# Loading the second batch's rows before the second weights of expert 3, with a margin for the sums of weights

## The chip, the cores and the metric

The kernel runs on one core of one Trainium2 chip. The metric is the device time of one execution in microseconds (us). The profile of each kernel is of one execution. The kernel before took 372.05 us in the median of the first three runs.

## The reference

The reference does two things one after the other: attention with a sliding window of 128 and four sink positions, and a mixture of four experts over all tokens, whose weights depend on the domain and not on the token's content.

```python
def _attn_ref(q, k, v, n_sink, window):          # B, H, S, D = 4, 8, 768, 64
    scores = scale * np.matmul(q, k.transpose(0, 1, 3, 2))
    keep = is_sink | in_window                   # 4 sinks, or 0 <= row - column < 128
    a = softmax of the kept scores               # written out in the original
    return np.matmul(a, v)

def _moe_ref(x, domain_probs, w1, w2):           # 3072 tokens, 512 wide, E = 4, F = 1024
    p = domain_probs / (domain_probs.sum(-1, keepdims=True) + 1e-09)
    for e in range(E):
        h = np.maximum(x @ w1[e], 0.0)
        out += p[:, e:e + 1] * (h @ w2[e])
```

The output of the attention, with heads side by side, is the input x of the mixture.

## The kernel before

The program is written by a scheduler in Python that is run once, when the kernel is built. It keeps a clock of its own (`t`, in ns) for each engine, estimates with it when data will have landed, and chooses by these estimates what TensorE does next. So there are two orders to watch. One is the order of the loads. The other is the order of the instructions on TensorE and VectorE, which follows from the estimates. A change in the first changes the estimates and so the second, although nothing is said about it in the code.

At the start of the main part, TensorE does the mixture of batch 0 while the inputs of batch 1 come in: rows of q and k (`load_nat`), a transposition of them by DMA (`turn_nat`), v (`load_v`). A batch has 768 rows, six blocks of 128; the kernel works in groups of two blocks, so I speak of the first, second and third pair. For some products the kernel also needs sums and differences of weights (`weight_form`, L294 to L300) and of tokens (L1052), which VectorE makes, and which are queued when the clock says that their inputs have landed.

```python
# --- the scheduler's own clock and its estimates, in ns ---
    t = {"pe": 1200.0, "act": 0.0, "dve": 0.0, "pool": 1280.0, "sp": 800.0, "sw": 6500.0, "hw": 0.0}
    ring, whole = [0.0] * 6, [False] * 6
    WARM = 6600.0
    FLIP, LATE = 300, 2500
    # ... cut ...
    def lands(key, rows, cols, *deps):
        issued = pool(0, *deps, fixed=880)
        t["sw"] = max(t["sw"], issued + 1500) + rows * ROW[cols] / 16
        landed[key] = t["sw"] + 900

    def sp(*deps, issue=530, takes=600):
        t["sp"] = max([t["sp"], *deps]) + issue
        at = max(t["hw"], t["sp"] + 800)
        t["hw"] = at + takes + max(0.0, min(takes, t["sw"] - at))
        return t["hw"] + 900
    # ... cut ...
# --- loads (gpsimd queue) and transpositions (sync queue) ---
    def load_nat(b, tb):
        both = sb.tile([P, 2, H, D], BF16, name="qkn", tag="qkn", bufs=NQB)
        for i, src in enumerate((q, k)):
            nc.gpsimd.dma_start(
                out=both[:, i], in_=src[b, :, tb * P:(tb + 1) * P, :].rearrange("h p d -> p h d"),
            )
            lands(("qk", b, tb), H * P, D, qkn_free[0])
        qkn_free.pop(0)
        qkn_free.append(1e12)
        nat[b, tb] = both

    def turn_nat(b, tb):

        if b not in qkT:
            qkT[b] = sb.tile([P, 2, NHP, S], BF16, name="qkT", tag="qkT", bufs=1)
        nc.sync.dma_start(
            out=qkT[b][:, :, :, tb * P:(tb + 1) * P].rearrange("c i h p -> c (i h) p"),
            in_=nat[b, tb].rearrange("p i h d -> p (i h d)"), transpose=True,
        )
        turned_at[b, tb] = sp(landed["qk", b, tb], scored_at.get(b - 1, 0.0), issue=1330, takes=1400) + LATE
        qkn_free.remove(1e12)
        qkn_free.append(turned_at[b, tb])
        qkn_free.sort()
    # ... cut: load_first, casts ...
    def load_v(b, ts):
        for tb in ts:
            nc.gpsimd.dma_start(
                out=vx[tb][:, :, 0:D],
                in_=v[b, :, tb * P:(tb + 1) * P, :].rearrange("h p d -> p h d"),
            )
            lands(("v", b, tb), H * P, D, values_at[b - 1, min(NG - 1, (tb + 1) // 2)] if b else 0.0)

    w1_sb, w2_sb = {}, {}
    # ... cut: load_w1, of the same kind ...
    def load_w2(e):
        w2_sb[e] = wpool.tile([P, NFB, Dout], BF16, name=f"w2_{e}", tag=f"w2_{e}")
        nc.gpsimd.dma_start(out=w2_sb[e], in_=moe_w2[e].rearrange("(fb p) d -> p fb d", p=P))
        lands(("w2", e), F, Dout)
    # ... cut ...
# --- sums of weights on VectorE: when may one be queued ---
    def form1_due(e):
        n = formed1.get(e, 0)
        if e >= OWN and turned_at.get((B - 1, NQB - 1), 1e12) > t["pe"]:
            return False
        return landed.get(("w1", e), 1e12) < t["pe"] and (n < 3 or n == 3 and not left1[e])

    def form_due(e):
        n = formed.get(e, 0)
        return landed.get(("w2", e), 1e12) < t["pe"] and (n < 3 or n == 3 and e in used)
    # ... cut ...
    def next_form():

        if forming:
            return False
        x = next(((weight_form1, e) for e in FAST if form1_due(e)), None) or next(
            ((weight_form, e) for e in range(E) if form_due(e)), None)
        if x is None:
            return False

        def run(engine):
            forming.clear()
            x[0](x[1])
        forming.append(x)
        later("dve", t["pe"], 9000, run)
        return True

    forms_at = {}
    # ... cut ...
# --- differences of tokens (only the test that the argument touches) ---
            at = max(xT_at.get((b, hp, g), 1e12) for hp in range(NHP))
            if at > t["pe"]:
                return
    # ... cut ...
# --- main loop: what is loaded, and when ---
        if not att.more() and not loaded:
            loaded = 1
            gates_by_row()
            loads += [(load_w1, 3), (load_w2, 3)]
            turns += [(1, tb) for tb in range(NQB)]
            for tb in range(NQB):
                loads.append((load_nat, 1, tb))
                if tb % 2:
                    loads += [(load_v, 1, (tb - 1,)), (load_v, 1, (tb,))]
        if loads and t["pool"] < now + 1500 and load_ready(loads[0]) < now + 1500 and free_ring(loads[0]):
            x = loads.pop(0)
            x[0](*x[1:])
        if turns and (ahead < 2 or not mix.second) and landed.get(("qk", *turns[0]), 1e12) < now and (turns[0][0] <= ahead or turns[0][0] == ahead + 1 and not att.todo):
            x = turns.pop(0)
            turn_nat(*x)
            # ... cut: queueing of the next batch ...
        flush(now)
        mix.tokens()
        mix.chore()
        if ahead:
            next_form()
        # ... cut: choice of the next step for TensorE ...
```

The softmax here doesn't subtract the row's maximum and nothing guards it: scores larger than these inputs give would overflow.

## Time and profile before

| kernel before | value |
|---|---|
| first three runs | 370.67 to 372.08 us, median 372.05 |
| profiled run | 369.88 us (span 368.1 us) |
| TensorE (PE) busy in the span | 357.2 us, 97% |
| w2 of expert 3 (w2[3]) landed | 61.38 us |
| last rows of batch 1 landed, transposed | 82.80, 87.49 us |

The page, the chain, TensorE's timeline and the stages are shown in the prediction below, and are not shown again. What they leave out is the short list of what TensorE waited for between 60 and 120 us, in the waits view of the kernel before. The columns are the engine, what waited, what ended the wait, and then the total in us, the number of waits, and the longest.

```profile
PE sinks L581 <- DMA qkT<-qkn: 0.7, 1, 0.7
PE acc L1303 <- DVE H L1015: 0.3, 1, 0.3
PE hps L1000 <- ACT aT L645: 0.2, 1, 0.2
PE acc L1303 <- issue: 0.2, 1, 0.2
```

(One more line, 0.2 us before the score products L620, on ScalarE, is cut.) The longest is the sinks' wait on the transposed rows. The last line has no releaser, only "issue"; its run of 512-column products at 83.92 us is x7, so one record is missing from it, and it is no wait. This view counts the time in which TensorE was idle; the 1.09 us of the prediction counts from the end of streaming of the product before, which is a little earlier than the modelled end of that product (by about 0.3 us at the last sinks). Below, "wait" means the second of these unless I say idle.

### The profile page before, as it was taken

The numbers are of one execution on the slowest core, as the hardware profiler recorded it, in microseconds if no ns is written. First come the engines' busy times: TensorE is split into PE (matmuls) and PEld (weight loads), VectorE is DVE, ScalarE is ACT, GpSimd is POOL, SyncE is SP. The second block draws the span as 40 slices with busy tenths as digits, with TensorE's granted clock in tenths as the row PEclk, the third lists the DMA queues.
The fourth block names the chain that finished last, engine by engine and source line by source line (L and its number), as shares of the span: only waits on it lengthen the run. The fifth ranks groups of instructions, "written<-read, shape, count | busy, mean of one in ns | idle before, by whom it ended". The sixth has DMA issues, their size and how long they took to land.

```text
span 368.1 us, 9866 instructions
## 1 busy us (share of the span) xinstructions
PE 357.2 (97%) x4107; PEld 297.1 (81%) x4119; DVE 283.3 (77%) x629; ACT 154.3 (42%) x397; POOL 71.2 (19%) x92
## 2 busy tenths in 40 slices
PE   6899999998999999999999999999999999999996
PEld 2575766765776788898888898899999999999995
DVE  5674997566543899789879979869898988898860
ACT  4764723369547155456444545452103213223110
POOL 8945113604901920010020000000000000000000
PEclk9999999999999999999999999999999999999999
DMA  9999999998999991518792131213002111020011
GB/s 164 173 189 199 210 212 179 144 147 143 167 159 231 176 150 31 86 46 86 142 147 73 16 102 30 45 45 86 16 19 85 30 45 60 16 74 2 2 59 57
DMA packets 117288, 37.20 MB, mean 101 GB/s; under 512 B 100612, under 2 KB 112740, under 8 KB 117244
## 3 DMA queue, kind: packets, MB, share of 16 engines
q0 software_dynamic: 77520, 17.31, 53.9%
q1 hardware_dynamic: 38668, 18.75, 23.6%
q8 instruction: 32, 0.52, 0.6%
q10 hardware_dynamic: 1056, 0.52, 0.5%
q14 instruction: 12, 0.10, 0.1%
HBM read 40.45 MB, written 6.34 MB: 127 GB/s over the span
## 4 chain that ended last, share of the span: by engine, by line
PE 69%; DMA 19%; POOL 5%; DVE 4%; issue 2%; ACT 1%; POOLq 0%; SPq 0%; DVEq 0%
PE acc L1232 29%; PE cps L1078 20%; PE hps L1000 13%; DMA w<-in_moe_w_dram 12%; DMA qkn<-in_k_dram 4%; PE acc L1303 3%; POOL qkn L191 2%; DMA xT<-onat 2%; PE od L686 2%; PE sps L620 2%; DMA qkT<-qkn 1%; POOL vx L256 1%; POOL w L269 1%; DVE H L1024 1%; PE od L679 1%
## 5 line engine op out<-in xcount | busy, mean ns | idle before, releaser
L1000 PE MATMUL hps<-xT,w 128*128 128x256 bf16 x768 | 95.0, 273 | 0.4 <-ACT aT L645 0.2
L1000 PEld LDWEIGHTS <-w 128*128 128x128 bf16 x768 | 73.0, 98 | 13.4 <-issue 2.2
L1232 PEld LDWEIGHTS <-H 128*128 128x128 bf16 x600 | 56.0, 98 | 6.5 <-issue 0.8
L645 ACT ACTIVATE aT<-sps 128x512 bf16<-128x512 f32 (+1 forms) x96 | 47.0, 579 | 26.7 <-PE sps L620 26.7
L1078 PEld LDWEIGHTS <-w 128*128 128x128 bf16 x768 | 48.3, 98 | 2.0 <-issue 0.5
L1232 PE MATMUL acc<-w,H 128*128 128x256 bf16 x360 | 48.0, 273 | 0.0
L725 ACT ACTIVATE onat<-od,R 128x64 bf16<-128x64 f32 x144 | 33.8, 327 | 32.6 <-DVE R L713 30.6
L1303 PE MATMUL acc<-w,H 128*128 128x512 bf16 x180 | 44.2, 379 | 1.1 <-issue 0.3
L1097 DVE SCALAR_TENSOR_TENSOR H<-cps,gates 128x512 bf16<-128x512 f32 x57 | 38.6, 683 | 2.2 <-PE cps L1078 1.2
L1275 ACT COPY osb<-acc 128x256 f32<-128x256 f32 x36 | 13.5, 375 | 58.2 <-PE acc L1232 56.0
L1013 ACT ACTIVATE H<-hps 128x512 bf16<-128x512 f32 x39 | 23.2, 599 | 34.5 <-PE hps L1000 34.3
L1024 DVE SCALAR_TENSOR_TENSOR H<-hps,gates 128x512 bf16<-128x512 f32 x44 | 30.0, 686 | 9.3 <-PE hps L1000 9.1
L256 POOL DMA_DIRECT2D vx<-in_v_dram x24 | 21.4, 909 | 60.4 <-PE od L686 49.2
L1303 PEld LDWEIGHTS <-H 128*128 128x128 bf16 x192 | 17.9, 98 | 18.6 <-DVE H L1015 0.8
L1232 PE MATMUL acc<-wf,H 128*128 128x256 bf16 x240 | 31.9, 273 | 0.0
L1232 PEld LDWEIGHTS <-S 128*128 128x128 bf16 x288 | 27.0, 98 | 3.1 <-issue 0.3
L1078 PE MATMUL cps<-T,w 128*128 128x128 bf16 x384 | 29.3, 219 | 0.0
L1078 PE MATMUL cps<-xT,w 128*128 128x128 bf16 x384 | 29.1, 219 | 0.0
L1106 ACT COPY cps<-cps 128x512 f32<-128x512 f32 x24 | 13.8, 576 | 33.1 <-PE cps L1078 31.0
L1078 PEld LDWEIGHTS <-vf 128*128 128x128 bf16 x432 | 26.9, 98 | 1.0 <-issue 0.3
L639 DVE TENSOR_TENSOR aT<-aT,mask 128x1024 bf16<-128x1024 bf16 (+1 forms) x36 | 22.7, 638 | 5.3 <-ACT aT L645 5.3
L1315 DVE SCALAR_TENSOR_TENSOR osb<-acc,scale_t,osb 128x512 f32<-128x512 f32 x18 | 13.5, 749 | 15.2 <-PE acc L1303 14.3
(116 smaller groups left out, 514.2 us busy)
## 6 DMA issues: line engine op xcount, KB each, us to landing
w<-in_moe_w_dram POOLq DMA_DIRECT2D x7, 1024.0 KB, 18.9
out_dram<-osb SPq DMA_DIRECT2D x23, 256.0 KB
gates<-gate_rows SPq DMA_DIRECT2D x36, 128.0 KB
vx<-in_v_dram POOLq DMA_DIRECT2D x24, 128.0 KB, 8.2
qkn<-in_q_dram POOLq DMA_DIRECT2D x22, 128.0 KB, 7.3
qkn<-in_k_dram POOLq DMA_DIRECT2D x22, 128.0 KB, 7.6
w<-in_moe_w_dram POOLq DMA_DIRECT2D x2, 512.0 KB, 8.3
kraw<-in_k_dram ACTq DMA_DIRECT2D x2, 256.0 KB
```

The source lines that it names most:

```text
L256: nc.gpsimd.dma_start(out=vx[tb][:, :, 0:D], in_=v[b, :, tb * P:(tb + 1) * P, :].rearrange("h p d -> p h d"),)
L639: nc.vector.tensor_mul(a, a, m[:, None, :].to_broadcast([P, 2, w]))
L645: nc.scalar.activation(out=a[:, ph], in_=sps[ph][:, 0:w], func=AF.Exp, scale=scale)
L725: nc.scalar.mul(o[:, qi, hp, ph * D:(ph + 1) * D], od[:, qi, ph, 0:D], R[:, qi, ph])
L1000: nc.tensor.matmul(h[:, i].rearrange("p (q n) -> p q n", q=2), lhsT=w1_sb[e][:, db, fb * P:(fb + 1) * P], rhs=xT[b, g][:, :, db], start=(i ...
L1013: nc.scalar.activation(out=dst, in_=h, func=AF.Relu)
L1024: nc.vector.scalar_tensor_tensor(out=dst, in0=h, scalar=0.0, in1=gate, op0=ALU.max, op1=ALU.mult,)
L1078: nc.tensor.matmul(y[:, f], lhsT=A[:, d, f * P:(f + 1) * P], rhs=T[:, d], start=(m in ("P1", "P5") and f == 0 and d == 0), stop=(d == 1), ...
L1097: nc.vector.scalar_tensor_tensor(out=dst, in0=src, scalar=0.0, in1=gate, op0=ALU.max, op1=ALU.mult)
L1106: nc.scalar.copy(out=tiles["Y"], in_=y)
L1232: nc.tensor.matmul(x, lhsT=self.operand(b, g, e, m)[:, f], rhs=forms[e][m][:, f], start=(k == 0 and f == 0 and m in (("P1", "P5", "P2") if ...
L1303: nc.tensor.matmul(op, lhsT=H[:, fb // QF, fb % QF, s], rhs=w2_sb[e][:, fb, :], start=(fb == 0), stop=(fb == NFB - 1),)
```

## The change

The intent: the rows and v of batch 1 are what the attention of batch 1 waits for, while w2[3] is needed only late, so the rows go first. Since w2[3] then lands later, the sums of its parts must not be queued before it is there: VectorE works in order, and a sum that stands on its weights holds all that is behind it. Therefore the diff also asks that a landing lies 4 us back on the scheduler's clock before a sum is queued.

```diff
--- before.py
+++ after.py
@@ -335,11 +335,11 @@
         n = formed1.get(e, 0)
         if e >= OWN and turned_at.get((B - 1, NQB - 1), 1e12) > t["pe"]:
             return False
-        return landed.get(("w1", e), 1e12) < t["pe"] and (n < 3 or n == 3 and not left1[e])
+        return landed.get(("w1", e), 1e12) + 4000 < t["pe"] and (n < 3 or n == 3 and not left1[e])
 
     def form_due(e):
         n = formed.get(e, 0)
-        return landed.get(("w2", e), 1e12) < t["pe"] and (n < 3 or n == 3 and e in used)
+        return landed.get(("w2", e), 1e12) + 4000 < t["pe"] and (n < 3 or n == 3 and e in used)
 
     forming = []
 
@@ -1367,12 +1367,13 @@
         if not att.more() and not loaded:
             loaded = 1
             gates_by_row()
-            loads += [(load_w1, 3), (load_w2, 3)]
             turns += [(1, tb) for tb in range(NQB)]
+            loads.append((load_w1, 3))
             for tb in range(NQB):
                 loads.append((load_nat, 1, tb))
                 if tb % 2:
                     loads += [(load_v, 1, (tb - 1,)), (load_v, 1, (tb,))]
+            loads.append((load_w2, 3))
         if loads and t["pool"] < now + 1500 and load_ready(loads[0]) < now + 1500 and free_ring(loads[0]):
             x = loads.pop(0)
             x[0](*x[1:])
```

## The prediction

> **What bounds the kernel now.** I read the page first (busy shares and the chain that ended last), then the chain in order of time between 27 and 92 us, then TensorE's and ScalarE's timelines there, and last the instruction order of the changed program against that of the kernel before. The page:
>
> ```profile
> PE 357.2 (97%) x4107; PEld 297.1 (81%) x4119; DVE 283.3 (77%) x629; ACT 154.3 (42%) x397; POOL 71.2 (19%) x92
> ...
> PE 69%; DMA 19%; POOL 5%; DVE 4%; issue 2%; ACT 1%; POOLq 0%; SPq 0%; DVEq 0%
> ```
>
> TensorE is busy in 97% of the span and holds 69% of the chain, but DMA holds 19%, so it looks as if earlier loads could pay. The chain in order of time shows where that DMA share lies:
>
> ```profile
> 29.98 31.40 DMA w<-in_moe_w_dram
> 61.38 0.28 issue
> 61.66 0.88 POOL qkn L191
> ...
> 69.08 13.72 DMA qkn<-in_k_dram
> 82.80 0.02 SPq L203
> 82.82 0.03 issue
> 82.85 4.64 DMA qkT<-qkn
> 87.49 0.14 issue
> 87.63 0.29 PE sinks L581 x4
> ```
>
> The second weights of expert 3 (I call them w2[3]) land at 61.38 us; behind them come the rows of batch 1, the last at 82.80; their transposition lands at 87.49; then TensorE may do the sink scores of batch 1. This is the load whose place the change alters. But a chain names one path, not how long TensorE waited on it. That is in TensorE's timeline (start, length, work, and in brackets the idle time before):
>
> ```profile
> 78.62 1.03 PE L1000 MATMUL hps<-xT,w 128*128 128x256 bf16 x8 [0.24 <-ACT aT L645]
> ...
> 83.09 0.67 PE L620 MATMUL sps<-qkT 64*128 64x128 bf16 x12 [0.15 <-ACT onat L725]
> 83.92 1.67 PE L1303 MATMUL acc<-w,H 128*128 128x512 bf16 x7 [0.16 <-issue]
> ...
> 86.33 0.55 PE L620 MATMUL sps<-qkT 64*128 64x128 bf16 x6
> 87.63 0.29 PE L581 MATMUL sinks<-qkT,ksd 128*32 128x256 bf16 x4 [0.75 <-DMA qkT<-qkn]
> ```
>
> The longest gap is the one on the transposed rows, and the others are on ScalarE. Between 61 and 75 us TensorE never waits: while w2[3] loads it does mixture work of batch 0. Stages of 5 us (busy time of PE, PEld, DVE, ACT, POOL) say why it waits on ScalarE:
>
> ```profile
> 80.00:85.00 5.00, 4.69 (x62) 3.49 (x61) 3.28 (x10) 4.95 (x20) 0.00 (x0) 1.00 1.82 182
> 85.00:90.00 5.00, 4.25 (x48) 2.27 (x47) 3.73 (x7) 4.99 (x16) 2.15 (x4) 1.00 0.64 113
> ```
>
> ScalarE is full (4.95 and 4.99 of 5.00) because attention of batch 1, late by then, is emitted almost without mixture work in between.
>
> **What can be won at all.** The program order of the changed kernel has exactly the same number of products of each shape, so the streaming time does not change. Start to start, a 256-column product takes 109 ns, a 128-column one 56, a 512-column one 216: 768 + 1008 of the first, 1344 of the second and 192 of the third are 193.6 + 75.3 + 41.5 = 310 us, and the attention products come on top. I took every gap from one start to the next less these times. From 40 to 366 us about 11 us are left. Gaps of 216 ns inside a run of 512-column products are records missing from the trace (the run is x7 instead of x8), and each visit to the half-height score products costs about 0.10 us going in and 0.11 coming out. What is left as true waiting after 75 us and up to 120 is: 1.09 us before the sinks at 87.63 (the six score products before it end streaming at about 86.5); on ScalarE 0.32 + 0.22 + 0.29 + 0.19 = 1.0 us, from the gaps before 78.62, 83.09, 83.92 and 91.65; and 0.48 us near 111 us, on VectorE. Together 2.6 us, 0.7% of the time. After 120 us nearly all of the remaining gaps are the visits to the score products.
>
> **What the Trainium skill says.** TensorE: Matmul & The Clock Gate, "Wait — 56ns, not 53.3ns?": a warm matmul starts N / 2.4 GHz + about 2.5 ns after the one before. The trace agrees (56, 109, 216 ns), so a group at this spacing has nothing to win. PSUM — Partial Sum Buffer, "Engine vs sequencer instructions": VectorE's queue is strict FIFO, so a sum whose weights have not landed holds up all evictions behind it. In the trace before this cannot be seen for w2[3], whose first sum starts at 64.59, 3.2 us after the landing. DMA: Bandwidth & Descriptors, "Issuing engines are not separate DMA queues": all loads run on the same 16 engines. The trace agrees: rows that land about 0.9 us apart while the queue is alone take 1.6 us and more apart when the transpositions run beside them. TensorEngine Tiling (Array Packing), "Key Properties": a change of tiling mode drains TensorE, which fits the 0.2 us per visit.
>
> **The change part by part.** (1) Rows and v of batch 1 go ahead of w2[3]. GpSimd's timeline has issues at 36.75, 41.97, 46.82, 51.83, 56.54 and 61.66 us, each let go by the landing of one weight transfer: a weight of 1 MB takes 4.7 to 5.2 us of the queue. So all 18 transfers of batch 1 move ahead by about 5.1 us: the last row from 82.80 to 77.7, its transposition from 87.49 to 82.4, and that of the second row block from 75.8 to 70.7. The changed order has the first scores 6.07 us of streaming time earlier in TensorE's program (24 products of 256 columns, 2.61 us, and 16 of 512, 3.46 us, now stand behind them), so at about 77.71 - 6.1 = 71.6 us: 0.9 us after their rows. The last sink scores stand 6.25 us of streaming later, near 92 us, ten us after their rows. So the 1.09 us wait goes entirely. The sinks and scores of the second group come at about 77.3 us against a landing at about 77.1: that can turn into a new wait of up to 1 us.
>
> (2) Attention is moved, hardly thinned. From the first scores to the last of the second group the changed order has 9.6 us of streaming, before 10.5; the mixture work in between is the same, four groups of eight 256-column products and two of eight 512-column ones, 6.9 us. ScalarE's program in that part is 8 exponentials at 0.40, 8 at 0.53, 20 small scalings at 0.235, a sink row 0.4 and one eviction 0.6: 3.2 + 4.2 + 4.7 + 0.4 + 0.6 = 13.1 us. TensorE, with about eight visits of 0.2 us, needs 9.6 + 1.6 = 11.2 us. So ScalarE stays full there and the fourth score pair, which needs its banks, waits near 83 us for about as long as before: of the 1.0 us I leave 1.0 us standing. Only after it, where the last two sinks used to follow, is there now mixture work.
>
> (3) w2[3] lands later. It starts when v is through, at 84.07 - 5.1 = 79.0, takes 5 us, and shares the engines with the last row transposition and that of the first attention output, about 2 us: 86 us. TensorE's first use of it (second products of expert 3) stands at the same place as before, about 101 us, so it has 15 us to spare. VectorE's first sum of it stands behind the fourth mask of the second group and is reached, with ScalarE as the pace (71.6 + 0.4 + 13.1, and a mask), near 85 us. The margin of 4 us in the queueing rule is counted on the program's own clock; by my estimate it falls short by about 1 us. VectorE then stands for that time, and TensorE, which still has free banks, loses perhaps 0.3 us of it.
>
> (4) The rest of the margin only delays sums of expert 0 to 2 by a step or two; nothing moves in TensorE's order for it. From the second products of expert 3 on, TensorE's order of the two programs is the same apart from one pair of scores, so what is won by 100 us is kept to the end.
>
> Sum: waits of 2.6 us become 0.48 (near 111 us, same order) + 1.0 (ScalarE) + 0.3 (second group of rows, an even chance of some 0.5) + 0.3 (VectorE behind w2[3]), near 2.0. The gain is 0.6 us; the three runs before have a median of 372.05 and a mean of 371.60, and from the middle of the two, 371.8, I come to 371.2 us.
>
> **The rivals.** First: the whole shift counts. The chain runs through the rows, they land 5.1 us sooner, so the kernel ends 5 us sooner, at 367. For it speaks the chain; against it that TensorE waited only 1.09 us for them, and that its streaming is fixed. The most it could gain, with every wait after 75 us gone, is 2.6 us: 369.4. Second: w2[3] lands much later than estimated, at 90 us or after, because of the transpositions beside it. VectorE then stands 5 us in its strict order with all reciprocals and evictions behind it, both accumulators fill, and TensorE loses 3 to 4 us: net 2 us slower, 374. For it speaks how the rows slowed (16 us for the last ten rows and v, where 9 would do); against it that most of the transpositions are over by 82 us. Third: nothing, because the new waits eat the old: 372.
>
> **Range and chances.** Central 371.2. Three runs of the kernel before spread over 1.4 us, and the rivals reach from 369.4 to 374, with the second less likely; 8 in 10 between 369.2 and 372.9. Faster by 2% needs 7.4 us where only 2.6 us of waits exist: 0.02. Slower by 2% needs VectorE held for over 8 us: 0.02. Within 2%: 0.96.
>
> **What would show it.** In the changed profile: first scores of batch 1 near 71.6 us; rows all landed near 78 us and w2[3] near 86; no wait of the sinks on transposed rows at the end of the burst; ScalarE still full (over 4.8 of 5 us) between 74 and 85, and some 2 us of TensorE waits there in place of 2.6; TensorE's second products of expert 3 starting 0.3 to 1.5 us sooner than 102.57. Step (3) is right if VectorE shows an idle stretch of 1 to 3 us before a sum of w2[3] (line 294), released by the weight transfer; wrong if there is none or if it exceeds 4 us. I am wrong as a whole if waits appear after 105 us that were not there, where both programs have the same order.

## The result, and the profile after

| | this (us) | range | before in the same rounds (us) | ratio |
|---|---|---|---|---|
| changed kernel | 369.66 | 369.15 to 370.00 | 371.83 | 0.9947 [0.9921, 0.9972] |

Ratios in this document are computed as the mean time of one kernel's runs over that of the other's of the same rounds, so they are not quite the ratio of the medians that stand beside them. By the ratio the changed kernel is half a per cent faster, about 2.0 us. The result was correct.

The profiled run of the changed kernel took 370.0 us, at the slow end of its runs, and that of the kernel before 369.88, at the fast end of its own. The two traces therefore do not show the gain as a difference of spans (368.3 and 368.1 us). They show the mechanism. First the page of the changed kernel, busy time and chain by engine:

```profile
PE 358.1 (97%) x4119; PEld 296.8 (81%) x4119; DVE 283.0 (77%) x629; ACT 154.4 (42%) x397; POOL 71.3 (19%) x92
...
PE 74%; DMA 17%; POOL 4%; DVE 3%; issue 1%; ACT 1%; POOLq 0%; DVEq 0%; SPq 0%; ACTq 0%
```

TensorE is as full as before. The chain goes from 69% on TensorE to 74%, and from 19% on DMA to 17%: a shift of several per cent in the chain, for half a per cent of time. The chain in order of time (start, length, what) shows where it leaves the transfers:

```profile
29.97 27.39 DMA w<-in_moe_w_dram
57.36 0.28 issue
...
59.52 9.84 DMA qkn<-in_k_dram
...
69.41 9.28 DMA qkT<-qkn
78.69 0.14 issue
78.82 0.32 PE sinks L581 x4
```

Before, the chain waited on weights until 61.38 us, and on rows until 87.49. Now the weights let go at 57.36 and the rows at 78.69, and it is the second pair of row blocks that the chain waits for, at the first sinks, not the last pair at the last sinks. TensorE's timeline shows both sinks (in brackets the idle time before):

```profile
71.66 0.51 PE L620 MATMUL sps<-qkT 64*128 64x256 bf16 x8
...
78.82 0.29 PE L581 MATMUL sinks<-qkT,ksd 128*32 128x256 bf16 x4 [1.59 <-DMA qkT<-qkn]
...
82.27 1.03 PE L1000 MATMUL hps<-xT,w 128*128 128x256 bf16 x8 [0.44 <-ACT onat L725]
...
94.82 0.29 PE L581 MATMUL sinks<-qkT,ksd 128*32 128x256 bf16 x4
```

The wait at the last sinks is gone: they come at 94.82, and their rows were there at 88.15. In exchange the first sinks wait 1.66 us (1.59 of it idle), where in the profiled run of the kernel before they did not wait. (They only just did not: their rows landed at 82.19 and they started at 82.35.) The stages in the same columns as in the prediction:

```profile
75.00:80.00 5.00, 3.41 (x39) 1.88 (x38) 1.90 (x7) 2.49 (x11) 0.00 (x0) 1.00 1.82 149
80.00:85.00 5.00, 4.56 (x52) 3.04 (x51) 3.01 (x6) 5.00 (x19) 0.00 (x0) 1.00 1.22 197
85.00:90.00 5.00, 5.00 (x53) 3.79 (x52) 3.02 (x6) 3.31 (x11) 1.50 (x3) 1.00 0.92 143
```

ScalarE is full from 80 to 85 us, but not from 74 on, as was predicted: from 75 to 80 it is busy for 2.49 us, since it idles 2.51 us until the first sinks give it their scores at 79.22. After 85 it is full no more (3.31 of 5.00, before 4.99), and TensorE is busy in all of 85 to 90. Last, VectorE's timeline around the landing of w2[3] at 87.00 us:

```profile
86.82 0.69 DVE L639 TENSOR_TENSOR aT<-aT,mask 128x1024 bf16<-128x1024 bf16 x1 [0.17 <-ACT aT L645]
87.43 0.68 DVE L294 TENSOR_TENSOR wf<-w 128x1024 bf16<-128x1024 bf16 x1
88.03 0.18 DVE L713 RECIPROCAL R<-od 128x4 f32<-128x4 f32 x1
90.57 0.29 DVE L1052 TENSOR_TENSOR T<-xT 128x256 bf16<-128x256 bf16 x1 [2.37 <-DMA xT<-onat]
```

The first sum of w2[3] (L294) started 0.43 us after the landing, with no idle time before it. The margin sufficed, barely: in the two copies the sum starts 0.45 and 0.03 us after the landing. VectorE does stand for 2.37 us, but before a difference of tokens, on the transposed output of the attention; TensorE's timeline has no wait that follows from it.

### The profile page after: what moved, and what is told of

Same layout as the page of the kernel before. It is cut to its first block, busy times and chain, and to the rows that moved or that the text cites. A ratio compares the mean times of both kernels' runs of the same rounds, so it can differ in the third digit from the quotient of the medians.

```text
span 368.3 us, 9878 instructions
## 1 busy us (share of the span) xinstructions
PE 358.1 (97%) x4119; PEld 296.8 (81%) x4119; DVE 283.0 (77%) x629; ACT 154.4 (42%) x397; POOL 71.3 (19%) x92
## 4 chain that ended last, share of the span: by engine, by line
PE 74%; DMA 17%; POOL 4%; DVE 3%; issue 1%; ACT 1%; POOLq 0%; DVEq 0%; SPq 0%; ACTq 0%
PE acc L1232 29%; PE cps L1078 20%; PE hps L1000 15%; DMA w<-in_moe_w_dram 11%; PE acc L1303 5%; DMA qkn<-in_k_dram 3%; DMA qkT<-qkn 3%; PE od L686 2%; PE sps L620 2%; POOL qkn L191 1%; POOL vx L256 1%; PE od L679 1%; ACT onat L725 1%; DVE H L1024 1%; POOL w L279 0%
## 5 line engine op out<-in xcount | busy, mean ns | idle before, releaser
L1000 PE MATMUL hps<-xT,w 128*128 128x256 bf16 x768 | 95.3, 273 | 0.4 <-ACT onat L725 0.4
L1000 PEld LDWEIGHTS <-w 128*128 128x128 bf16 x768 | 72.8, 98 | 13.8 <-issue 2.7
L1303 PE MATMUL acc<-w,H 128*128 128x512 bf16 x192 | 45.4, 379 | 0.0
L639 DVE TENSOR_TENSOR aT<-aT,mask 128x1024 bf16<-128x1024 bf16 (+1 forms) x36 | 22.7, 641 | 7.3 <-ACT aT L645 7.3
```

Source lines behind the costliest of these rows:

```text
L639: nc.vector.tensor_mul(a, a, m[:, None, :].to_broadcast([P, 2, w]))
L1000: nc.tensor.matmul(h[:, i].rearrange("p (q n) -> p q n", q=2), lhsT=w1_sb[e][:, db, fb * P:(fb + 1) * P], rhs=xT[b, g][:, :, db], start=(i ...
L1303: nc.tensor.matmul(op, lhsT=H[:, fb // QF, fb % QF, s], rhs=w2_sb[e][:, fb, :], start=(fb == 0), stop=(fb == NFB - 1),)
```

## The experiments

Twelve kernels ran, in three calls of four, each call on one chip with runs of the kernel before among them. All results were correct. To compare what the traces lose and gain I also use the time from TensorE's 193rd to its 385th 256-column product of L1000, which start at 64.1 to 66.4 us and at 122.5 to 131.1. The work between these is the same in all the kernels, and it holds everything that the change moves.

| label | what it is | this (us) | before (us) | ratio [95%] | stretch (us) |
|---|---|---|---|---|---|
| (first profile) | before | | | | 58.23 |
| (first profile) | changed | 369.66 | 371.83 | 0.9947 [0.9921, 0.9972] | 58.40 |
| c_before | copy of before | 371.12 | 370.54 | 1.0004 [0.9978, 1.0031] | 58.86 |
| c_after | copy of changed | 369.81 | 370.54 | 0.9971 [0.9954, 0.9989] | 58.08 |
| e_order | loads moved, no margin | 377.18 | 370.54 | 1.0170 [1.0146, 1.0194] | 67.02 |
| e_margin | margin, loads not moved | 370.83 | 370.54 | 0.9996 [0.9975, 1.0016] | 59.95 |
| e_blate | before, rows estimated 2 us later | 368.92 | 370.64 | 0.9949 [0.9926, 0.9973] | 57.16 |
| e_m2 | changed, margin of 2 us | 375.12 | 370.64 | 1.0133 [1.0102, 1.0164] | 62.09 |
| e_mid | changed, w2[3] after row block 4 | 376.55 | 370.64 | 1.0143 [1.0114, 1.0173] | 64.81 |
| e_late3 | changed, later rows estimated 2 us later | 371.05 | 370.64 | 1.0009 [0.9982, 1.0037] | 61.13 |
| e_late3t | e_late3, token differences queued later | 368.03 | 370.88 | 0.9922 [0.9897, 0.9946] | 56.23 |
| c_after2 | copy of changed | 370.27 | 370.88 | 0.9986 [0.9961, 1.0010] | 58.69 |
| e_blate2 | e_blate again | 368.96 | 370.88 | 0.9950 [0.9926, 0.9973] | 57.14 |
| e_bl4 | before, rows estimated 4 us later | 368.84 | 370.88 | 0.9938 [0.9912, 0.9964] | 57.13 |

My theory was that the gain is the wait on the rows, less a new and smaller one. The rivals were that the gain comes from the sums' new places on VectorE and not from the loads; that it is only a matter of runs; and, later, that it comes from the place of the attention in TensorE's program and not from the rows landing sooner.

### c_before: the kernel before once more

No edit. It was to show how much the waits of one program vary from run to run.

> The kernel before, unchanged, against itself, for a second trace and the noise of a ratio. Theory A (the gain is the wait of the last sink scores of batch 1 on their transposed rows, and its size varies from run to run with the landing of the rows): ratio 1.000 within 0.003; in the trace the last transposed rows land later than the 87.49 us of the first trace, by some 1 to 2 us, and the wait before the sinks is longer by the same amount than the 1.09 us there; the span is longer than 368.1 us by about as much. Theory B (the runs differ by their first 40 us, and the measured gain of 2.2 us is partly luck): the sinks are reached with a wait near 1.1 us as before, and a longer span comes from the stretch up to 40 us.

The time is that of the kernel before, as it should be: 1.0004. The trace is not. Its timeline of TensorE has both sinks waiting:

```profile
83.84 0.29 PE L581 MATMUL sinks<-qkT,ksd 128*32 128x256 bf16 x4 [0.64 <-ACT onat L725]
...
89.57 0.29 PE L581 MATMUL sinks<-qkT,ksd 128*32 128x256 bf16 x4 [1.43 <-DMA qkT<-qkn]
```

The last sinks wait 1.43 us idle (1.75 from the end of streaming) where the first profile had 0.75 (1.09), and the first sinks 0.71 where it had none. The rows landed later: w2[3], ahead of them in the queue, at 63.13 us here and at 61.38 in the first profile. (The view puts the first of these waits on ScalarE. The transposition of the fourth block landed at 83.70, and the sinks started 0.14 us after it, as in the other traces; ScalarE's scalings ended just then, at 83.81, but in the first profile the same sinks started at 82.35 with these scalings running until 83.04, so they do not need the last of them. It is the rows.) So the prediction, which took its removable wait from a single trace, took it from a lucky one. The difference between the two runs is there early: the first landing of weights is at 16.30 us in the first profile and at 17.57 here, and lies between 16.22 and 17.77 in all traces. What makes it so stays open. Of the 1.4 us by which this span is longer, 0.8 us are there before the stretch begins (at 66.24, not 65.46) and 0.6 are in it, so both theories of the expectation have a part.

### c_after and c_after2: the changed kernel twice more

No edit. One copy ran in the first call and one in the third, beside the experiments that they are compared with.

> The changed kernel, unchanged, timed in more rounds, with a second trace. Theory A: 0.993 to 0.997 of the kernel before; a wait of 0.5 to 2 us before the first sinks of batch 1 (on the second pair of row blocks) and none before the last. Theory B: 0.997 to 1.001, and the wait of the first sinks is about as large as the one removed.

> The changed kernel again, on the same chip as the two beside it: 0.994 to 0.998 of the kernel before, a wait of 1.3 to 1.8 us before the first sinks, runs within 1 us.

Three calls give the ratios 0.9947, 0.9971 and 0.9986; the first two exclude 1, the third does not. Their mean is 0.9968, about 1.2 us. The traces agree with the first one: the last sinks do not wait in any of the three, the first sinks wait 1.66, 1.28 and 1.46 us. The runs of the changed kernel also agree better with one another (369.71 to 370.10 us) than those of the kernel before (369.62 to 372.87 for its copy). In the third call they do not agree within 1 us as expected (369.81 to 371.38), and the ratio 0.9986 is outside the expected 0.994 to 0.998.

### e_margin: the margin alone

The kernel before with the two `+ 4000` and with its own order of loads.

```diff
-        return landed.get(("w2", e), 1e12) < t["pe"] and (...)
+        return landed.get(("w2", e), 1e12) + 4000 < t["pe"] and (...)    # and the same for w1
```

> Only the margin, loads in their old order. TensorE's order is that of the kernel before instruction for instruction; five sums on VectorE move by a few places near 65 us, where VectorE is idle for a third of the time. Theory A: ratio 1.000 within 0.003. Theory D (the margin by itself gives the gain): 0.993 to 0.997.

The ratio is 0.9996: the margin by itself gives nothing. TensorE's order is exactly that of the kernel before, and five sums moved on VectorE. Its trace is also a third look at the waits of that order: 1.21 us at the first sinks, 1.58 at the last. The theory that the sums' new places make the gain falls.

### e_order: the moved loads alone

The changed kernel without the two `+ 4000`.

```diff
-        return landed.get(("w2", e), 1e12) + 4000 < t["pe"] and (...)
+        return landed.get(("w2", e), 1e12) < t["pe"] and (...)           # and the same for w1
```

> Only the loads moved, without the margin. VectorE's first sum of the second weights of expert 3 now stands nine instructions earlier, ahead of an eviction of an accumulator and of the last three masks of the second group. Theory A (the margin is what keeps VectorE from standing in front of a load that has not landed): VectorE idles 4 to 8 us before that sum until the landing near 87 us, TensorE loses 3 to 6 us of it, and the kernel is slower than the changed one by that and slower than before by 1 to 4 us: 1.003 to 1.010. Theory C (the margin does nothing, VectorE has slack): equal to the changed kernel within 0.002, 0.993 to 0.997.

It is 1.7% slower than the kernel before, more than the 0.3 to 1.0% that was expected, and 7.4 us slower than the copy of the changed kernel (377.18 less 369.81). VectorE's timeline says why:

```profile
86.49 0.69 DVE L294 TENSOR_TENSOR wf<-w 128x1024 bf16<-128x1024 bf16 x1 [9.62 <-DMA w<-in_moe_w_dram]
```

The first sum of w2[3] was queued too early, and VectorE stood 9.62 us on it. A mask of the attention (L639) stood behind it, and TensorE needed that mask, as its timeline shows:

```profile
88.50 0.40 PE L686 MATMUL od<-vx,aT 128*128 128x65 bf16 x4 [4.96 <-DVE aT L639]
89.04 5.02 PE L1000 MATMUL hps<-xT,w 128*128 128x256 bf16 x24
```

TensorE waited 4.96 us and then did 24 products in 5.02 us, for which it takes 2.78 at its usual pace: another 2.2 us. (The mean granted clock of this run was 0.991: it was 0.50 from 86.81 to 93.63 us.) The Trainium skill, TensorE: Matmul & The Clock Gate, "What's actually happening", says that the clock of TensorE falls back to 1.2 GHz, half of its full rate, after an idle window of about 3.4 us; this trace agrees, with a gap of 4.96 us: 5.02 us for 24 products is 209 ns each, where 2.78 us is 116. 4.96 and 2.2 are nearly the whole loss. The margin alone is worth nothing, but with the moved load it is what keeps the change from being a loss of 6.6 us.

### e_m2: half the margin

```diff
-        ... + 4000 < t["pe"] ...
+        ... + 2000 < t["pe"] ...
```

> The changed kernel with a margin of 2 us in place of 4. The first sum of the second weights of expert 3 stands behind the first mask and the eviction that ended at 82.8 us in the changed kernel, ahead of two evictions and three masks. Theory A: VectorE idles 3.5 to 5 us before it, until about 87 us; TensorE loses 1 to 3.5 us and some more where its granted clock falls: 1.000 to 1.008 of the kernel before, between the changed kernel and the one without margin. Theory C (a threshold lies below 2 us): as the changed kernel, 0.994 to 0.998.

A margin of 2 us is not enough: 1.0133, above the expected 1.000 to 1.008. VectorE stands 4.3 us before L294 (a line of its waits view), and TensorE waits for an eviction that stands behind it (its timeline):

```profile
DVE wf L294 <- DMA w<-in_moe_w_dram: 4.3, 1, 4.3
```

```profile
88.18 1.91 PE L1000 MATMUL hps<-xT,w 128*128 128x256 bf16 x16 [3.52 <-DVE H L1015]
```

Here 16 products after 3.52 us of idleness took 1.91 us, the usual pace, so this run did not pay with its clock (its mean granted clock was 1.0). It was the fastest of its runs (373.33 us, where the others go up to 377.43). The others have no trace, but the record gives their mean granted clock: 0.990 to 0.995 in all five. So most runs of this kernel did pay with the clock as well. Between a margin of 4 us and one of 2 us lies a loss of 1.6% (from 0.9971 in the first call to 1.0133 here); where in between it begins was not tried, and the two ratios are of different calls.

### e_mid: w2[3] in the middle of the rows

If w2[3] were loaded after four of the six row blocks, VectorE would have it sooner and the first two pairs would still be early. The experiment also asks what a transfer of 1 MB beside the transpositions does to them.

```diff
         for tb in range(NQB):
             ...
                 if tb % 2:
                     loads += [(load_v, 1, (tb - 1,)), (load_v, 1, (tb,))]
+                if tb == 3:
+                    loads.append((load_w2, 3))
-            loads.append((load_w2, 3))
```

> The changed kernel with the second weights of expert 3 loaded between the fourth and the fifth row block of batch 1, not behind the sixth. They should land 8 to 10 us sooner, near 77 to 79 us; the last rows land 5 us later but their sinks have 6.7 us of slack in the changed kernel's trace. Theory A: the first sinks wait as in the changed kernel (1.2 to 1.9 us), the last do not, VectorE stands at most 1.5 us for the weights: 0.994 to 0.999. If all rows must be ahead for the gain, a wait of over 1 us before the last sinks and 0.999 to 1.004.

It is 1.4% slower, which neither of the two expectations foresaw: w2[3] landed at 81.87 us instead of 77 to 79, VectorE stood 4.09 us for it, and the long wait came before the first sinks, not the last. The chain in order of time, and TensorE's timeline where it ends:

```profile
68.71 14.79 DMA qkT<-qkn
83.50 0.14 issue
```

```profile
83.64 0.41 PE L581 MATMUL sinks<-qkT,ksd 128*32 128x256 bf16 x4 [6.30 <-DMA qkT<-qkn]
...
84.52 3.60 PE L1303 MATMUL acc<-w,H 128*128 128x512 bf16 x8
```

The transposition of the fourth row block took 14.79 us, and landed only after w2[3]. The same block took 9.3 us in the changed kernel, beside loads of rows and v alone; the shortest transpositions in the traces take 3.1 us (one in the kernel before runs from 108.92 to 112.02). The sinks waited 6.30 us for it, and again the products after that ran at half the pace (3.60 us for eight of 512 columns, usually 1.89). In the changed kernel the same is seen in the fifth block: issued at 76.18, when its rows had landed, and itself landed at 87.29, 11.1 us later and after w2[3] at 87.00; in the kernel before the same block took 5.8 us. So of the two later places that were tried, the last one, which the change chose, is where w2[3] does the rows less harm.

### e_blate, e_blate2 and e_bl4: only the scheduler's estimate

The loads and the rule for sums stay those of the kernel before; what is changed is that the scheduler believes that the transposed rows of batch 1 land 2 us later (4 us in e_bl4). No transfer moves earlier. The attention of batch 1 only comes later in TensorE's program, behind mixture work.

```diff
-        turned_at[b, tb] = sp(landed["qk", b, tb], scored_at.get(b - 1, 0.0), issue=1330, takes=1400) + LATE
+        turned_at[b, tb] = sp(landed["qk", b, tb], scored_at.get(b - 1, 0.0), issue=1330, takes=1400) + LATE + (2000 if b == 1 else 0)
```

> The kernel before with its loads and sums as they were; only the program's own estimate of when a transposition of batch 1's rows lands is set 2 us later, so the scheduler puts the first sink scores 1.9 us and the last 3.8 us of streaming later in TensorE's order. Theory A (the kernel before loses time because TensorE's order reaches the sinks before the rows, by 1.1 to 2.9 us in its traces): no wait of the sinks on transposed rows over 0.3 us, 0.993 to 0.998 of the kernel before, and runs that agree within 1 us. Theory E (the earlier loads give something else, which a later place in the order can't): 0.998 to 1.003, with new waits, or the same on ScalarE.

> The kernel before with the estimate for batch 1 set 2 us later, again, beside the changed kernel on one chip. Theory A (both take away the same waits): both ratios between 0.993 and 0.998 and within 0.002 of each other. If moving the loads gives something more: the changed kernel ahead by over 0.002.

> The kernel before with the estimate for batch 1 set 4 us later. Theory A: no wait of TensorE on transposed rows in any case, even where the rows land 2 us later than in the first trace, and attention of batch 1 still early enough for what follows: 0.993 to 0.998. If attention is then too late for the first units of batch 1: a wait of TensorE after 105 us and 0.998 to 1.003.

The ratios are 0.9949, 0.9950 and 0.9938. TensorE's timeline of e_blate has the sinks without a wait:

```profile
85.03 0.29 PE L581 MATMUL sinks<-qkT,ksd 128*32 128x256 bf16 x4
...
91.64 0.29 PE L581 MATMUL sinks<-qkT,ksd 128*32 128x256 bf16 x4
```

What the waits view still lists from 60 to 120 us is 0.4 us on ScalarE (in e_bl4, 0.5 on VectorE at 110.48). The runs of e_blate agree less well than expected: within 1.7 us, not 1. So no load has to move to get the gain. These two kernels are ahead of the copy of the changed one (0.9950 and 0.9938 against 0.9986). The 95% intervals just overlap, so the times alone do not settle that they are faster. The stretch gives 57.14 and 57.13 us against 58.69; the 1.5 us between are about what the first sinks wait in the changed kernel (1.46 in that trace). I had expected the estimate alone to come within 0.002 of the change, and it came out 0.0036 ahead, most likely for that reason. I read the change in the same way, which is an inference: it too puts the attention further behind the rows that it needs, by moving the rows instead. It does not get all of the gain: its first sinks come too soon. That is tested next.

### e_late3: the first sinks of the changed kernel, later

If that is so, the changed kernel should gain by an estimate that is 2 us later for the blocks from the third on, so that the sinks wait no more.

```diff
-        turned_at[b, tb] = sp(landed["qk", b, tb], scored_at.get(b - 1, 0.0), issue=1330, takes=1400) + LATE
+        turned_at[b, tb] = sp(landed["qk", b, tb], scored_at.get(b - 1, 0.0), issue=1330, takes=1400) + LATE + (2000 if b == 1 and tb > 1 else 0)
```

> The changed kernel, with the estimate of when the transpositions of the third to sixth row block of batch 1 land set 2 us later; the first sinks move 2.6 us of streaming later. Theory A: their wait of 1.3 to 1.7 us goes, 0.990 to 0.996 of the kernel before and 1 to 1.7 us faster than the changed kernel. Rival F: VectorE's order now has the token differences of the first attention output, which landed at 90.6 us in the changed kernel, ahead of the fourth mask; it stands for it 2 to 4 us and TensorE gives the gain back: 0.996 to 1.001.

It did not gain: 1.0009. The wait of the first sinks is gone, but TensorE has new ones, 1.8 us on a mask and 1.2 us on an eviction, both of VectorE. VectorE's timeline shows what both stood behind:

```profile
90.76 0.29 DVE L1052 TENSOR_TENSOR T<-xT 128x256 bf16<-128x256 bf16 x1 [5.08 <-DMA xT<-onat]
90.97 0.68 DVE L639 TENSOR_TENSOR aT<-aT,mask 128x1024 bf16<-128x1024 bf16 x1
```

The first difference of tokens (L1052) was now queued ahead of the mask, and stood 5.08 us on the transposed output of the attention, which was issued at 84.00, while w2[3] was still loading (it landed at 87.22), and landed at 90.74. In the changed kernel the same difference stood 2.37 us, but with nothing urgent behind it. The two new waits are not all: from 94.31 to 97.72 us the granted clock of this trace is 0.50, and 16 products from 94.25 take 3.55 us instead of 1.91. No single gap before it was longer than 1.75 us; from 90.90 to 94.31 TensorE was idle for 2.00 us in all. The trace is of the slowest run of this kernel (373.03 us, median 371.05), so its stretch of 61.13 us is longer than usual.

### e_late3t: the same, with that difference later

```diff
-            if at > t["pe"]:
+            if at + (5000 if (b, g) == PAIRS[0] else 0) > t["pe"]:
```

> The changed kernel with the 2 us on the estimate for the third to sixth row block as in the last experiment, and the four token differences of the first attention output queued 5 us later, so they stand behind all masks of the second group again. If rival F is right in that VectorE's 5.1 us wait for that output was what gave the gain back: VectorE waits under 2.5 us for it with no TensorE wait on a mask, TensorE's wait before the first sinks stays gone, and 0.990 to 0.996 of the kernel before, 0.5 to 1.7 us faster than the changed kernel. If the later sinks are bad for another reason: 0.999 to 1.003 again.

TensorE's order is that of e_late3, product for product. Only VectorE's order differs: the mask and the sums of w2[3] now come before the differences.

```profile
86.18 0.66 DVE L639 TENSOR_TENSOR aT<-aT,mask 128x1024 bf16<-128x1024 bf16 x1
86.76 0.69 DVE L294 TENSOR_TENSOR wf<-w 128x1024 bf16<-128x1024 bf16 x1
...
89.82 0.29 DVE L1052 TENSOR_TENSOR T<-xT 128x256 bf16<-128x256 bf16 x1 [0.32 <-DMA xT<-onat]
```

The ratio is 0.9922, and the stretch falls from 61.13 to 56.23 us (about 1.6 of these 4.9 us are the half clock in the trace of e_late3). TensorE's list of waits from 60 to 120 us is empty; its sinks come at 80.51 and 93.39 without a wait. This is the fastest kernel and beats both: the kernel before by 2.9 us, and the changed one, whose interval ([0.9961, 1.0010]) lies above its own ([0.9897, 0.9946]). From e_bl4 and e_blate2 the intervals do not separate it.

## Why the prediction was right or wrong

The time lay within the predicted range and on the predicted side of the 2% line, 1.5 us below the predicted 371.2 us. The main claim of the prediction was right: the load's 5 us are not what is won, only TensorE's true waits are. Its terms fared differently, several were wrong, and three signs that it named did not come.

- **The wait on the rows that is removed, 1.09 us.** It was mis-sized, because it came from one trace. The three traces with this order of TensorE have 1.09, 1.75 and 1.58 us at the last sinks, and 0, 0.71 and 1.21 at the first; together 1.09, 2.46 and 2.79, in the mean 2.1. (Counted as idle time: 0.75, 2.07 and 2.41, in the mean 1.7.) That the last sinks would not wait at all after the change held in all three traces of it.
- **The new wait at the second pair, 0.3 us expected.** It was 1.66, 1.28 and 1.46 us, in the mean 1.5 (idle: 1.4). The step that failed is the landing at 77.1 us, by a shift of 5.1 us from 82.19: it was 78.69, a shift of 3.5 us in the first pair of profiles. The run of the changed kernel had begun later (w1[3] landed at 57.36, before at 56.25), which is 1.1 of the missing 1.6 us. In the mean of three traces each the landing moves from 83.11 to 78.55 us, by 4.6: the 82.19 from which I started was early, like the wait of 1.09. The first scores were predicted at 71.6 and came at 71.66. So TensorE's program was placed well, and the transfers were not.
- **ScalarE, 1.0 us left standing.** The 1.0 us was misread. Of its four gaps the 0.29 us before 83.92 is no wait: the run behind it is x7, and the 216 ns of the missing record, with about 0.1 for leaving the score products, are the whole gap. So 0.7 us stood there in the first trace, and by the same count 0.5 in the two others of this order; in the three traces of the changed kernel it is 0.5. ScalarE did not change much. It also was not the pace from 74 us on, as I had taken it to be: it idled 2.51 us until the first sinks, and after 85 us it was full no more. That TensorE's wait before the group is what gave it time is argued, not tested; the two traces of the old order in which the first sinks wait point the same way (0.5 us against 0.7), but the difference is small.
- **w2[3] at 86 us, VectorE idle before its first sum, 0.3 us lost.** It landed at 87.00, close. VectorE was not idle: it reached the sum at 87.43 instead of near 85, most likely since the first sinks' wait had pushed all of it back. The prediction named an idle stretch of 1 to 3 us there as a sign, and that sign did not come. The danger was real all the same: with 2 us less margin (e_m2) it is 1.3% slower than the kernel before, with none (e_order) 1.7%.
- **The last transposition at 82.4 us.** It was at 88.15. I had let the transpositions follow their rows as before, and w2[3] now runs beside the last two. It did no harm, since the last sinks come at 94.82.
- **The 0.48 us near 111 us, to stay.** They are gone in all three traces of the changed kernel; one of them (c_after2) has 0.57 us on VectorE at 93.24 instead. Of the three traces of the old order two have them (0.48 and, in e_margin, 0.70). It is not a fixed cost of the order.
- **The other signs.** TensorE's second products of expert 3 were to start 0.3 to 1.5 us sooner than 102.57 us. They started at 103.30, 0.7 us later, because the first trace of the kernel before was an early one: with the copies (104.51 and 104.08 before, 103.14 and 103.56 after) the means are 103.72 and 103.33, 0.4 us sooner. And ScalarE, which was to be full from 74 to 85 us, was so only from 80 on.

The sum: 2.6 us of waits were to become 2.0, a gain of 0.6 us. The traces give about that: the two sinks together go from a mean of 2.1 us to 1.5 (idle: from 1.7 to 1.4), ScalarE hardly changes, and the stretch goes from a mean of 59.0 us in the three traces of the old order to 58.4, by 0.6. That the sum came out is partly luck: the wait that went was 1.0 us larger than predicted, and the new one 1.2 us larger. And three traces each, whose stretches differ by up to 1.7 us, are few for 0.6 us. The ratios of the three calls mean 1.2 us, from 0.5 to 2.0; the rest of the distance to 371.2 lies in the runs of the kernel before from which I started (median 371.83 in the first call, 370.54 to 370.88 in the others).

Of the rivals, the first (the whole shift counts, 367 us) is refuted by the time and by c_after. The second (w2[3] at 90 us or after) did not come, with a landing at 87.00; its mechanism is that of e_order and e_m2. The third (nothing) is excluded in two calls and not in the one with c_after2. What no rival named is that the gain needs no moved load at all.

## What to carry to other kernels

Where one engine is full in 97% of the span, a shift of the chain's transfers is worth only that engine's own waits, and their sizes should be read from several traces: here the wait on the rows in one order of TensorE went from 1.1 to 2.8 us with the run. In a program that is ordered by estimates, try first to change an estimate by itself; here 2 us in one line did at least as much as moving eighteen transfers. When a load is moved back, look at all that stands behind its first user in a queue that works strictly in order, and at what runs beside it on the transfer engines.

## What the Trainium skill lacked or had wrong

- DMA: Bandwidth & Descriptors, "Issuing engines are not separate DMA queues", says that transfers of all issuers interleave on the same engines. The runs agree. The page tells how the engines take turns between queues, but gives no measure of what a large load does to a transposition beside it: here one took 14.79 us (e_mid, where the same block takes 9.3 beside rows alone) and one 11.1 us (changed kernel; 5.8 before), and both landed only after the 1 MB of weights. The shortest take 3.1 us.
- TensorEngine Tiling (Array Packing), "Key Properties", says that a change of mode drains TensorE, and gives no time. Here a visit to the half-height score products costs about 0.2 us in all (0.10 going in, 0.09 to 0.11 coming out), worked out from start-to-start times in the kernel before.
- TensorE: Matmul & The Clock Gate, "What's actually happening", lets the clock fall after at least one idle window of about 3.4 us. After gaps of 4.96 us (e_order) and 6.30 us (e_mid) the granted clock was indeed halved, but so it was in e_late3, where no gap was longer than 1.75 us and TensorE was idle for 2.00 us of the 3.41 us before. After a single gap of 3.52 us (traced run of e_m2) it was not. So a window need not be wholly idle. Elsewhere the page tells of short idle times with this effect, but gives no figure; where the limit lies these runs do not show either.
- No page that I read says how much the first landings vary between executions of one program; here 16.22 to 17.77 us. In the three traces of the old order (16.30, 17.46 and 17.57) the waits on the rows differ by up to 1.7 us, more than the whole effect of the change.
